# Cosine attention and a two-layer network in one kernel: the first eighteen pairs in another order, three loads in two parts, fewer products of zeros

## The chip, the cores and the metric

The kernel runs on one core of one Trainium2 chip. The metric is the time of one execution in microseconds (us), from the device. A core has five engines that run their own instruction queues in order: TensorE (PE, matrix products; its loads of the stationary operand are listed as PEld), VectorE (DVE), ScalarE (ACT), GpSimd (POOL) and SyncE (SP, which here only issues transfers). Sixteen DMA engines move data between HBM and SBUF.

## The reference

```python
q_n = q / (norm(q, axis=-1) + 1e-06);  k_n = k / (norm(k, axis=-1) + 1e-06)
scores = matmul(q_n, k_n.transpose(0, 1, 3, 2)) / tau
attn = softmax(scores)
x = matmul(attn, v)                      # (8, 12, 448, 64), then (3584, 768)
h = x @ w_in                             # (3584, 2048)
g = h * clip(h + 3.0, 0.0, 6.0) / 6.0
out = g @ w_out                          # (3584, 768)
```

Eight batches, twelve heads, 448 positions, head dimension 64, tau 0.1; all inputs and the output are float32.

## The kernel before

**Pairs.** Heads h and h+6 of a batch are a pair, so there are 48 pairs, six to a batch. An item is the queries or the keys of two neighbouring pairs: 128 partitions by 14 rows of 64 numbers (two heads by seven columns c). Items 0 to 13 alternate: item 0 is the queries of pairs 0 and 1, item 1 their keys, item 2 the queries of pairs 2 and 3, item 3 their keys, and so on. In all there are 48 items.

**Steps of an item.** LQ loads it (SP, 448 KB, `load_qk`, L199). SQ squares it by columns on POOL or ACT (L225, L227), RE sums the squares on DVE (L242); BN and BS do the same for a few columns on DVE by moments (L248, L253, L254). NO makes the inverse norms of an item or of both items of two pairs: Ln and Exp on ACT (L278, L279), then either Ln and Exp again on ACT (L284, L285) or, with "v", a sum and a reciprocal on DVE (L281, L282). NM multiplies the item by its inverse norms into bfloat16 (`normalise`, L295), whole or by heads (".0", ".1"), on DVE or POOL. TR transposes it on PE into a PSUM bank (L341), and CQ and CK copy queries and keys of one pair to SBUF, with CS for the last 64 keys (`copy`, L361 on ACT, L363 on DVE).

**Steps of a pair.** SC are the scores, products of keys and queries in four groups 0 to 3 (L441, L444). EX are the exponentials (ACT, L462): for pairs 0 to 5 one instruction of 896 columns for each of three groups and one of 448, from two double banks SC; from pair 6 on, where a ring of six single banks is opened (OPEN), seven of 448 columns. LV loads values (four transfers for two pairs, L214), VC casts them (L312 on DVE, L314 on POOL or ACT). VA multiplies with the values into the bank PV (L484), FI divides by the sums (DVE, L504, L505), BK transposes back (L518) and CX copies into x (L361, L363).

**The network.** W issues one load of weights from POOL's queue (L924). U issues a unit of the first layer (six products of 448 columns, L594) or of the second (L754, L834); UH issues a part of a first-layer unit of batch 0 while its pairs are still being made; UA and UV are the work on ACT and DVE behind a unit (L611, L617). GS and WS are sums that the second layer's scheme of fewer products needs.

**Products of zeros.** DP.n issues n products of a zero tile into unused columns of PV (248 columns, bfloat16, L937); DQ.n does so with the zeros taken as float32, which the trace lists as two records each; D.n uses 512 columns and the bank Y (L931). Nothing reads what they write.

**What sets the order.** The program for pairs 0 to 17 is written out by hand in `PLAN`, a list of such steps: `LQ.1` loads item 1, `SQ.1.p.3.2` squares two columns of item 1 from column 3 on POOL, `SC.6.0` is group 0 of pair 6. The instructions of each engine run in the order in which the plan names them, so a step that waits holds up all steps behind it on its engine. `run` reads the plan; from pair 18 on a loop sets the order, which the change leaves alone. Names ".Y" and ".Z" in the plan pick a PSUM bank; without them `bank_of` takes the next of the ring.

Of the kernel before, what the change touches and what calls it, by code (L numbers as in the profile page):

```python
# [64 lines left out]
def kernel(
# [125 lines left out]
    def load_qk(j, *heads):  # L191
        needs(("NM", raw_before(j)))
        raw_of[j] = raw_buffer(j)
        d = j // 2
# [4 lines left out]
        nc.sync.dma_start(out=raw_of[j][:, g, :, :].rearrange("p g c d -> p g (c d)"), in_=f[:, g, :])  # L199
# [16 lines left out]
    def square(j, e, c0, n):  # L216

        needs(("RE", j - 2), ("LQ", j, 0), ("LQ", j, 1))
        if j not in sq_of:
# [4 lines left out]
        if e == "a":
            nc.scalar.activation(out=o, in_=i, func=AF.Square)  # L225
# [29 lines left out]

    def norms(d, *items):
        on_vector, items = "v" in items, tuple(x for x in items if x != "v")
# [2 lines left out]
        items = items or (0, 1)  # L260
# [2 lines left out]
        it = slice(items[0], items[-1] + 1)
        inverse([t[:, d % 2, it, :] for t in n2_and_r], nr_eps[:, d % 2, it, :, :], on_vector)
# [3 lines left out]
    def norms_two(d, on_vector=None):  # L268

        needs(*(("NM", 2 * d + x) for x in range(-4, 0)), *(("RE", 2 * d + x) for x in range(4)))  # L270
        two = [t.rearrange("p e i c -> p (e i) c") for t in n2_and_r]
        inverse(two, nr_eps.rearrange("p e i c x -> p (e i) c x"), on_vector)
        issued.update(("NO", x, y) for x in (d, d + 1) for y in range(2))

    def inverse(tiles, pairs, on_vector):
# [3 lines left out]
        nc.scalar.activation(out=nr, in_=ln, func=AF.Exp, scale=0.5)  # L279
        if on_vector:  # L280
            nc.vector.tensor_reduce(out=le, in_=pairs, axis=AX.X, op=ALU.add)  # L281
            nc.vector.reciprocal(out=r, in_=le)  # L282
        else:
            nc.scalar.activation(out=le, in_=nr, func=AF.Ln, bias=eps_bias)  # L284
            nc.scalar.activation(out=r, in_=le, func=AF.Exp, scale=-1.0)  # L285

    def normalise(j, e, *heads):
# [7 lines left out]
        engines[e].tensor_tensor(  # L295
            out=nrm[:, :, g, :].rearrange("p c g d -> p g c d"),
            in0=raw_of[j][:, g, :, :],
            in1=n2_and_r[2][:, d % 2, j % 2, :]
            .rearrange("p (g c) -> p g c", g=2)[:, g, :]
            .to_broadcast([128, n, 7, D]),  # L300
# [18 lines left out]
    def bank_of(name, reads):  # L319

        bank = {"Y": Y, "Z": Z}[name] if name else next_bank()
# [796 lines left out]
```

## Time and profile before

| | us |
|---|---|
| median of 3 runs | 400.86 (400.78 to 400.98) |
| the profiled execution | 401.17 |
| its span, first to last instruction | 399.2 |
| busy in the span: PE / DVE / ACT / POOL | 390.2 / 293.9 / 276.9 / 234.6 |

The granted clock of TensorE was 1.000 over the span. A row of the timeline gives the start, the time from the start of the first to the end of the last of the merged instructions, engine, line, operation, tiles, form and count; in brackets stands the idle time of the engine before it, and what ended that. A row of busy time by stretch gives, for a stretch of the span, its length, then for each engine the busy time and the count of instructions. Lines are those of the kernel before; in the changed kernel the same code stands some 5 to 53 lines further down.

### The profile page before, as it was taken

The numbers are of one execution on the slowest core, as the hardware profiler recorded it, in microseconds if no ns is written. First come the engines' busy times: TensorE is split into PE (matmuls) and PEld (weight loads), VectorE is DVE, ScalarE is ACT, GpSimd is POOL, SyncE is SP. The second block draws the span as 40 slices with busy tenths as digits, with TensorE's granted clock in tenths as the row PEclk, the third lists the DMA queues.
The fourth block names the chain that finished last, engine by engine and source line by source line (L and its number), as shares of the span: only waits on it lengthen the run. The fifth ranks groups of instructions, "written<-read, shape, count | busy, mean of one in ns | idle before, by whom it ended". The sixth has DMA issues, their size and how long they took to land.

```text
span 399.2 us, 9590 instructions
## 1 busy us (share of the span) xinstructions
PE 390.2 (98%) x3658; PEld 231.6 (58%) x3658; DVE 293.9 (74%) x537; ACT 276.9 (69%) x600; POOL 234.6 (59%) x234
## 2 busy tenths in 40 slices
PE   7999999999999999999999999999999999999996
PEld 5566556555565556555565556565565556555563
DVE  7998898999777787667767886686756566645663
ACT  5999889895768677777868769668648755235230
POOL 6999628662656988389368757767666400400070
PEclk9999999999999999999999999999999999999999
DMA  8999979988978868785887566795953423230133
GB/s 289 310 221 240 212 226 248 199 189 208 197 172 187 120 174 162 174 213 123 195 202 213 136 152 155 165 218 119 190 150 69 102 48 68 47 74 20 30 71 97
DMA packets 93165, 63.73 MB, mean 160 GB/s; under 512 B 56128, under 2 KB 93120, under 8 KB 93120
## 3 DMA queue, kind: packets, MB, share of 16 engines
q1 hardware_dynamic: 87408, 56.45, 60.4%
q0 software_dynamic: 5312, 6.29, 9.4%
q8 instruction: 28, 0.46, 0.5%
q10 hardware_dynamic: 400, 0.39, 0.3%
q14 instruction: 17, 0.14, 0.1%
HBM read 45.61 MB, written 11.01 MB: 142 GB/s over the span
## 4 chain that ended last, share of the span: by engine, by line
PE 92%; ACT 3%; DVE 2%; DMA 1%; issue 0%; POOL 0%; SPq 0%; DVEq 0%; ACTq 0%
PE M L594 25%; PE M L754 17%; PE PV L484 11%; PE Z L594 6%; PE Y L754 6%; PE M L444 5%; PE Y L594 5%; PE Z L754 5%; PE M L834 3%; ACT at L462 2%; DMA big<-in_k_dram 1%; PE Y L444 1%; PE Z L444 1%; PE Z L834 1%; PE PV L937 1%; PE SC L444 1%
## 5 line engine op out<-in xcount | busy, mean ns | idle before, releaser
L594 PE MATMUL M<-xT,w_in_sb 128*128 128x448 bf16 x540 | 114.6, 353 | 0.0
L462 ACT ACTIVATE at<-M 128x448 bf16<-128x448 f32 x195 | 96.6, 564 | 20.0 <-PE M L444 10.2
L594 PEld LDWEIGHTS <-w_in_sb 128*128 128x128 bf16 x768 | 72.2, 98 | 64.1 <-issue 3.8
L227 POOL TENSOR_TENSOR big<-big 128x896 f32<-128x896 f32 (+5 forms) x47 | 69.5, 1483 | 21.7 <-DMA big<-in_k_dram 12.0
L295 POOL TENSOR_TENSOR nrm<-big,r 128x896 bf16<-128x896 f32 (+1 forms) x45 | 75.7, 1683 | 6.5 <-ACT r L285 4.3
L617 DVE SCALAR_TENSOR_TENSOR gT<-u,M 128x448 bf16<-128x448 bf16 x80 | 49.0, 619 | 34.9 <-ACT u L611 34.3
L611 ACT ACTIVATE u<-M,bias 128x448 bf16<-128x448 f32 x90 | 58.0, 651 | 22.3 <-PE M L594 20.9
L484 PEld LDWEIGHTS <-at 128*128 128x128 bf16 (+1 forms) x1536 | 53.8, 97 | 20.5 <-issue 10.6
L484 PE MATMUL PV<-vx,at 128*128 128x65 bf16 (+1 forms) x1536 | 62.2, 193 | 0.0
L242 DVE TENSOR_REDUCE n<-big 128x14 f32<-128x896 f32 (+1 forms) x48 | 51.1, 1068 | 1.5 <-POOL big L227 1.5
L783 POOL TENSOR_TENSOR big<-big 128x384 f32<-128x384 f32 x12 | 13.0, 1080 | 58.9 <-ACT big L802 58.8
L401 POOL COPY km<-tT 64x128 bf16<-64x128 bf16 x34 | 12.8, 376 | 59.0 <-DMA tT<-nrm 24.9
L754 PEld LDWEIGHTS <-gT 128*128 128x128 bf16 x320 | 30.9, 98 | 21.4
L505 DVE TENSOR_TENSOR on<-PV,rc 128x512 bf16<-128x512 f32 x48 | 33.2, 692 | 1.7
L754 PEld LDWEIGHTS <-gs 128*128 128x128 bf16 x248 | 23.9, 98 | 16.0 <-issue 0.2
L462 ACT ACTIVATE at<-Y 128x448 bf16<-128x448 f32 x51 | 28.7, 564 | 6.1 <-PE Z L444 6.0
L754 PE MATMUL M<-w_out_sb,gT 128*128 128x384 bf16 x176 | 32.2, 326 | 0.0
L444 PE MATMUL M<-tT,kz 64*128 64x448 bf16 (+1 forms) x175 | 31.6, 351 | 0.3 <-ACT at L462 0.3
L462 ACT ACTIVATE at<-Z 128x448 bf16<-128x448 f32 x48 | 26.9, 561 | 4.2 <-PE M L444 2.1
L754 PE MATMUL M<-w_sum,gs 128*128 128x384 bf16 (+1 forms) x168 | 29.1, 318 | 0.0
L594 PE MATMUL Z<-xT,w_in_sb 128*128 128x448 bf16 x132 | 28.6, 352 | 0.0
L729 DVE TENSOR_TENSOR gs<-gT 128x1024 bf16<-128x1024 bf16 x30 | 26.3, 876 | 0.0
(135 smaller groups left out, 562.3 us busy)
## 6 DMA issues: line engine op xcount, KB each, us to landing
big<-in_k_dram SPq DMA_DIRECT2D x24, 448.0 KB, 4.4
big<-in_q_dram SPq DMA_DIRECT2D x24, 448.0 KB, 4.4
out_dram<-o SPq DMA_DIRECT2D x107, 96.0 KB, 2.2
big<-in_v_dram SPq DMA_DIRECT2D x48, 128.0 KB, 4.1
big<-in_v_dram SPq DMA_DIRECT2D x48, 96.0 KB, 4.1
w_in_sb<-in_moe_w_in_dram POOLq DMA_DIRECT2D x8, 384.0 KB, 8.3
w_out_sb<-in_moe_w_out_dram POOLq DMA_DIRECT2D x4, 768.0 KB, 11.0
tT<-nrm SPq DMA_TRANSPOSE x34, 3.2
```

Of the source, the lines that this page charges most:

```text
L227: engines[e].tensor_tensor(out=o, in0=i, in1=i, op=ALU.mult)
L242: nc.vector.tensor_reduce(out=sums_of(j, c0, n), in_=sq[:, :, c0 : c0 + n, :], axis=AX.X, op=ALU.add)
L295: engines[e].tensor_tensor(out=nrm[:, :, g, :].rearrange("p c g d -> p g c d"), in0=raw_of[j][:, g, :, :], in1=n2_and_r[2][:, d % 2, j % 2, :]
L444: nc.tensor.matmul(o, ks, qt[rows], start=True, stop=True)
L462: nc.scalar.activation(out=o, in_=x, func=AF.Exp, scale=inv_tau)
L484: nc.tensor.matmul(pv_out(j, h), at[rows, n, q_cols(i // HP, j)], vt[rows, 3 + h if name == "M" else 5 * h + int(name[1]), :], start=(name ...
L505: nc.vector.tensor_tensor(out=on[:, :, :, :].rearrange("p j h d -> p h j d"), in0=pv4[:, :, :, 0:D], in1=rc[:, :, :].to_broadcast([128, 2, ...
L594: nc.tensor.matmul(ps[:, 0:S], w_in_sb[:, cc, fc * 128 : (fc + 1) * 128], xT[b % 2][:, cc, 0:S], start=(cc == 0), stop=(cc == CC - 1), ski ...
L611: nc.scalar.activation(out=u[:, :], in_=ps[:, 0:S], func=AF.Relu, bias=half_bias, scale=1.0 / 6.0)
L617: nc.vector.scalar_tensor_tensor(out=g[:, fc, c0 : c0 + S], in0=u[:, :], scalar=1.0, in1=ps[:, 0:S], op0=ALU.min, op1=ALU.mult,)
L729: nc.vector.tensor_tensor(out=o[:, :, :], in0=x, in1=y, op=op)
L754: nc.tensor.matmul(m, lhs[:, c, :], rhs[:, c, c0 : c0 + width], start=(base is None and c == 0), stop=(c == KC - 1), skip_group_check=True,)
```

## The change

The plan of pairs 0 to 17 is another one. What the diff below shows, in words:

- `load_qk` can load a part of the columns of an item (before: of its heads). Item 0 is loaded as columns 2 to 6 and then 0 and 1, item 3 as 4 to 6 and then 0 to 3, item 4 as 2 to 6 and then 0 and 1. Squares need only their own columns.
- NO is split into NA (the two steps on ACT) and NV (the other two), so that other work can stand between them.
- There are 9 products DP and 14 products DQ (before: 47 DP, 9 DQ, one D). All but four of them (DQ.1, DP.1 and DP.2 after the first scores) stand before the first scores; before, 40 of the DP stood behind them.
- Steps change engines, among others these. To ACT: all squares of items 1 (the columns not made by moments) and 5, the casts VC.5 and VC.8, CK.8, CX.2, the squares of items 16 (six columns) and 19. To DVE: CK.0, CQ.0, CX.0, VC.3, two columns of item 6 by moments. To POOL: half of NM.1, half of NM.2 and of NM.4, VC.0, NM.11, NM.12, more columns of item 15.
- The order of the whole list is another one. Among others NV.0.0, the inverse norms of item 0, stands behind SQ.2.a.0.4 on ACT; NM.1.p.0 and NM.0 follow each other on POOL; three weight loads W stand ahead of NM.6 and NM.7; UH.0.0 stands ahead of SC.7.1.
- `RING` writes out which PSUM bank each step takes, in place of the names in the plan.
- The code can also put inverse norms into PSUM for a `NM.w`; the plan has no such step.

```diff
 PLAN = [
-    "LQ.1 BN.1.0.3 DQ.9 SQ.1.p.3.2 SQ.1.a.5.2 BS.1.0.3 LQ.0 RE.1.3.4 SQ.0.p.0.3 LQ.3 SQ.3.p.0.4 SQ.0.a.3.4 RE.0 LQ.2",
-    "NO.0.1 NM.1.v.0 NM.1.v.1 SQ.3.a.4.3 NO.0.0 NM.0.p.1 SQ.2.a.4.3 TR.1.Z NM.0.p.0 LQ.5 SQ.2.a.0.4 D.1 DP.1 RE.3",
-    "CK.0.a SQ.5.p.0.4 SQ.5.a.4.3 RE.2 NO.1.v TR.0.Y LQ.4 CQ.0.a SQ.4.p.4.3 DP.2 SQ.4.a.0.4 DP.3 NM.3.p DP.1 RE.5",
-    "CQ.1.v RE.4 LV.0 SC.0.0.0 LQ.6 DP.3 VC.0.v NM.2.v.1 EX.0.0 SC.0.1.1 NM.2.p.0 CK.1.v LQ.7 LQ.8 DP.5 EX.0.1",
-    "SC.0.2.0 EX.0.2 DP.1 VC.1.v DP.1 DP.1 SC.0.3.1 EX.0.3 DP.2 VA.0.0 DP.2 LV.1 SQ.6.p.0.7 VA.0.1 SC.1.0.0 NO.2.v",
-    "NM.4.v.1 SC.1.1.1 TR.2.Y DP.1 NM.4.p.0 SQ.7.a.4.3 DP.1 RE.6 DP.1 DP.1 EX.1.0 EX.1.1 SC.1.2.0 TR.3.Z EX.1.2",
-    "CK.2.v DP.1 CQ.2.v SQ.7.p.0.4 DP.1 DP.1 VA.0.2 VA.0.3 SQ.8.a.4.3 NM.5.p SC.1.3.1 VC.3.p LQ.10 FI.0 EX.1.3 LQ.9",
...
-    "SC.3.2.0 DP.1 VA.2.2 VA.2.3 RE.9 SQ.11.p.0.7 CK.4.v NM.7.p EX.3.1 SC.3.3.1 EX.3.2 SC.4.0.0 EX.3.3 BK.0.Z FI.2",
-    "DP.1 RE.10 VA.3.0 W NO.4.v CK.5.v DP.1 RE.11 CX.0.a DP.2 LQ.12 SC.4.1.1 EX.4.0 TR.6.Z SC.4.2.0 NM.9.p VC.5.p W",
...
-    "CK.7.v VA.4.0 EX.5.3 VA.4.1 OPEN CS.7.v SC.6.0 EX.6.0 VA.4.2 VA.4.3.t CS.6.v FI.4 SC.6.1 EX.6.1 SC.6.2 SC.6.3",
...
+    "LQ.1 LQ.0.2.5 LQ.0.0.2 SQ.1.a.3.2 SQ.1.a.5.2 SQ.0.p.2.1 BN.1.0.3 LQ.3.4.3 SQ.0.p.0.2 RE.1.3.4 BS.1.0.3",
+    "SQ.0.a.3.4 RE.0.4.3 LQ.3.0.4 NA.0.1 RE.0.0.4 NV.0.1 LQ.2 LQ.5 SQ.3.a.0.4 SQ.3.p.4.3 NA.0.0 NM.1.v.1 SQ.2.a.0.4",
+    "NV.0.0 RE.3.0.4 SQ.2.a.4.3 LQ.4.2.5 NM.1.p.0 RE.2.0.3 DQ.10 DP.3 TR.1 RE.3.4.3 RE.2.3.4 CK.0.v CK.1.v NM.0.p",
+    "SQ.5.a.4.3 LQ.4.0.2 NA.1 NV.1.v SQ.4.a.0.4 SQ.5.a.0.4 LV.0 DQ.3 DP.1 TR.0 SQ.4.p.4.3 LQ.6 CQ.0.v RE.4 LQ.8",
+    "RE.5.0.7 LV.1 NM.3.p VC.1.v DP.2 SC.0.0.0 VC.0.p EX.0.0 SC.0.1.1 EX.0.1 DQ.1 DP.1 SC.0.2.0 TR.3 NM.2.p.0 EX.0.2",
+    "CQ.1.v NM.2.p.1 LQ.7 BN.6.0.2 BS.6.0.2 SQ.6.p.2.5 LV.2 NA.2 SC.0.3.1 NV.2.v VC.2.v VA.0.0 EX.0.3 CK.2.v SC.1.0.0",
+    "EX.1.0 DP.2 SC.1.1.1 VA.0.1 EX.1.1 SC.1.2.0 EX.1.2 TR.2 NM.4.p.1 SQ.7.p.0.4 VA.0.2 VA.0.3 CQ.2.v SQ.7.a.4.3",
...
+    "SC.2.3.1 RE.7.0.7 LQ.10 CQ.3.v VA.1.0 LQ.9 SQ.8.a.0.4 EX.2.2 VC.3.v TR.5 W VA.1.1 VA.1.2 EX.2.3 RE.8 SQ.9.a.0.4",
+    "SC.3.0.0 SQ.9.p.4.3 CK.4.v NA.3 W EX.3.0 VA.1.3.t LV.3 FI.1 RE.9 SQ.10.p.0.7 SC.3.1.1 TR.4 EX.3.1 CQ.5.v W",
+    "VA.2.0 LQ.11 NA.4 NV.3.v VA.2.1 CQ.4.v SC.3.2.0 VC.4.v SC.3.3.1 VA.2.2 EX.3.2 VA.2.3 EX.3.3 SC.4.0.0 SC.4.1.1",
+    "SQ.11.p.0.7 NM.6.p VC.5.a LQ.12 EX.4.0 FI.2 EX.4.1 VA.3.0 CK.5.v NM.7.p.1 BK.0 SC.4.2.0 VA.3.1 VA.3.2 EX.4.2",
+    "RE.11 BK.2 CX.2.a SC.4.3.1 VA.3.3.t SC.5.0.0 EX.4.3 EX.5.0 TR.6 NM.7.p.0 SC.5.1.1 RE.10 CX.0.v NV.4.v TR.7",
+    "EX.5.1 FI.3 CQ.7.v SC.5.2.0 EX.5.2 CK.6.v SC.5.3.1 EX.5.3 OPEN NA.5 VA.4.0 VA.4.1 VA.4.2 CQ.6.v LQ.13 VA.4.3.t",
+    "SC.6.0 CS.6.v SC.6.1 NM.8.p EX.6.0 CK.7.v EX.6.1 BK.3 CS.7.v SC.6.2 W BK.1 FI.4 EX.6.2 NV.5.v VA.5.0 CX.3.v",
...
-    def load_qk(j, *heads):
+    def load_qk(j, *part):
...
-        g = slice(heads[0], heads[0] + 1) if heads else slice(0, 2)
-        nc.sync.dma_start(out=raw_of[j][:, g, :, :].rearrange("p g c d -> p g (c d)"), in_=f[:, g, :])
+        c0, w = part or (0, 7)
+        o = raw_of[j][:, :, c0 : c0 + w, :].rearrange("p g c d -> p g (c d)")
+        nc.sync.dma_start(out=o, in_=f[:, :, c0 * D : (c0 + w) * D])
...
     def norms(d, *items):
+        norms_root(d, *items)
+        norms_inverse(d, *items)
...
+    def root(tiles, pairs):
         n2, le, r = tiles
         ln, nr = n2, pairs[:, :, :, 0]
         nc.scalar.activation(out=ln, in_=n2, func=AF.Ln)
         nc.scalar.activation(out=nr, in_=ln, func=AF.Exp, scale=0.5)
```

More of the change, by code (lines that the diff above doesn't have):

```diff
@@ L21 @@
 PLAN = [
[39 rows of a table removed]
-]
[40 rows of a table added]
+]
+PLANNED = " ".join(PLAN).split()
+RING = "232323322345012345012345012340123012345234501234501234012350123450123450123450123450123501234501345012345012345012345012345012345012345012345012"
 @with_exitstack
@@ L216, in square @@
     def square(j, e, c0, n):
-        needs(("RE", j - 2), ("LQ", j, 0), ("LQ", j, 1))
+        needs(("RE", j - 2), *(("LQ", j, c) for c in range(c0, c0 + n)))
         if j not in sq_of:
@@ L244, in moments @@
     def moments(j, c0, n):
-        needs(("RE", j - 2), ("LQ", j, 0), ("LQ", j, 1))
+        needs(("RE", j - 2), *(("LQ", j, c) for c in range(c0, c0 + n)))
         for c in range(c0, c0 + n):
@@ L254, in sums_of_moments, with norm_tiles, inverses, in_psum @@
         nc.vector.scalar_tensor_tensor(out=sums_of(j, c0, n), in0=mean, scalar=1.0, in1=m2, op0=ALU.mult, op1=ALU.add)
+    def norm_tiles(d, items):
+        items = tuple(x for x in items if x != "v") or (0, 1)
+        it = slice(items[0], items[-1] + 1)
+        return items, [t[:, d % 2, it, :] for t in n2_and_r], nr_eps[:, d % 2, it, :, :]
     def norms(d, *items):
[L257 removed]
+        norms_root(d, *items)
+        norms_inverse(d, *items)
+    def inverses(j, g):
+        n = j // 2 % 2 * 2 + j % 2
+        c = slice(7 * g, 7 * g + 7)
+        if any(x in PLANNED for x in (f"NM.{j}.w", f"NM.{j}.w.{g}")):
+            return PV[:, 1, 264 + 14 * n : 278 + 14 * n][:, c]
+        return n2_and_r[2][:, j // 2 % 2, j % 2, c]
+    def in_psum(j):
+        return [any(x in PLANNED for x in (f"NM.{j}.w", f"NM.{j}.w.{g}")) for g in range(2)]
+    def norms_root(d, *items):
         needs(("NM", 2 * d - 4), ("NM", 2 * d - 3))
[L260 removed]
+        items, tiles, pairs = norm_tiles(d, items)
         for x in items:
             needs(("RE", 2 * d + x))
[L263 to L264 removed]
+        root(tiles, pairs)
+    def norms_inverse(d, *args):
+        items, tiles, pairs = norm_tiles(d, args)
+        le, r = tiles[1:]
+        parts = [(le, r)]
+        if any(any(in_psum(2 * d + x)) for x in items):
+            parts = []
+            for n, x in enumerate(items):
+                h = in_psum(2 * d + x)
+                n7 = PV[:, 1, 264 + 14 * (d % 2 * 2 + x) : 278 + 14 * (d % 2 * 2 + x)]
+                if h[0] == h[1]:
+                    parts.append((le[:, n, :], n7 if h[0] else r[:, n, :]))
+                else:
+                    for g in (0, 1) if h[0] else (1, 0):
+                        c = slice(7 * g, 7 * g + 7)
+                        parts.append((le[:, n, c], n7[:, c] if h[g] else r[:, n, c]))
+        inverse(tiles, pairs, "v" in args, parts)
         for x in items:
@@ L270, in norms_two @@
         needs(*(("NM", 2 * d + x) for x in range(-4, 0)), *(("RE", 2 * d + x) for x in range(4)))
+        assert not any(any(in_psum(2 * d + x)) for x in range(4))
         two = [t.rearrange("p e i c -> p (e i) c") for t in n2_and_r]
-        inverse(two, nr_eps.rearrange("p e i c x -> p (e i) c x"), on_vector)
+        pairs = nr_eps.rearrange("p e i c x -> p (e i) c x")
+        root(two, pairs)
+        inverse(two, pairs, on_vector)
         issued.update(("NO", x, y) for x in (d, d + 1) for y in range(2))
-    def inverse(tiles, pairs, on_vector):
+    def root(tiles, pairs):
         n2, le, r = tiles
@@ L279, in inverse @@
         nc.scalar.activation(out=nr, in_=ln, func=AF.Exp, scale=0.5)
+    def inverse(tiles, pairs, on_vector, parts=None):
+        n2, le, r = tiles
+        nr = pairs[:, :, :, 0]
+        parts = parts or [(le, r)]
         if on_vector:
             nc.vector.tensor_reduce(out=le, in_=pairs, axis=AX.X, op=ALU.add)
-            nc.vector.reciprocal(out=r, in_=le)
         else:
             nc.scalar.activation(out=le, in_=nr, func=AF.Ln, bias=eps_bias)
-            nc.scalar.activation(out=r, in_=le, func=AF.Exp, scale=-1.0)
+        for x, o in parts:
+            if on_vector:
+                nc.vector.reciprocal(out=o, in_=x)
+            else:
+                nc.scalar.activation(out=o, in_=x, func=AF.Exp, scale=-1.0)
     def normalise(j, e, *heads):
@@ L294, in normalise @@
         n = len(heads)
+        assert e == "w" or not any(in_psum(j)[x] for x in heads)
+        if n == 1 or e == "w":
+            r = inverses(j, heads[0]) if n == 1 else PV[:, 1, 264 + 14 * (j % 4) : 278 + 14 * (j % 4)]
+        else:
+            r = n2_and_r[2][:, d % 2, j % 2, :]
         engines[e].tensor_tensor(
@@ L319, in bank_of @@
     def bank_of(name, reads):
[L321 removed]
+        bank = next_bank()
         key = id(bank)
@@ L924, in next_weights @@
         nc.gpsimd.dma_start(out=o, in_=w)
-    def busy(n):
-        bank_of("Y", 0)
-        for _ in range(n):
-            nc.tensor.matmul(Y[:, :], zeros[:, 0:128], zeros[:, :], start=True, stop=True)
     def busy_pv(n, z=None):
```

22 lines of the change are left out of this document (10 added, 12 removed), and 55 rows, old and new, of the table PLAN.

## The prediction

> **What bounds the kernel now.** I read the summary of the span first, then the table of busy time by stretch, then the early part of the timeline engine by engine, then the landing times of the first loads.
>
> ```profile
> span 399.2 us, 9590 instructions
> PE 390.2 (98%) x3658; PEld 231.6 (58%) x3658; DVE 293.9 (74%) x537; ACT 276.9 (69%) x600; POOL 234.6 (59%) x234
> ```
>
> TensorE (PE) is busy for nearly the whole span. But part of that is work that counts for nothing, the products of zeros at L937. The next two views part the stages: all instructions first, then L937 alone (columns: stretch, its length, busy PE, PEld, DVE, ACT, POOL with counts, granted clock, DMA share, GB/s; in the second only PE and PEld).
>
> ```profile
> 7.50:12.70 5.20, 2.83 (x27) 1.67 (x26) 4.61 (x7) 4.55 (x13) 4.93 (x5) 1.00 1.08 325
> 12.70:20.00 7.30, 7.18 (x84) 4.33 (x85) 7.20 (x15) 7.11 (x13) 7.30 (x7) 1.00 1.04 320
> 20.00:28.00 8.00, 7.65 (x115) 5.28 (x115) 7.77 (x17) 7.84 (x16) 7.98 (x7) 1.00 0.91 211
> 28.00:34.50 6.50, 5.81 (x89) 3.72 (x87) 6.25 (x19) 6.45 (x11) 6.48 (x7) 1.00 1.11 274
> 34.50:43.00 8.50, 8.38 (x163) 6.10 (x164) 6.18 (x21) 7.77 (x17) 8.48 (x11) 1.00 1.13 209
> 43.00:60.00 17.00, 16.93 (x166) 9.14 (x159) 16.02 (x32) 14.91 (x33) 6.35 (x6) 1.00 0.97 222
> 60.00:105.00 45.00, 44.95 (x445) 25.46 (x444) 41.89 (x76) 37.42 (x81) 27.58 (x27) 1.00 1.00 207
> ```
> ```profile
> 12.30:20.00 7.70, 3.51 (x22) 1.67 (x22) 1.00 1.04 322
> 20.00:28.00 8.00, 2.35 (x13) 1.03 (x13) 1.00 0.91 211
> 28.00:34.50 6.50, 0.80 (x5) 0.32 (x4) 1.00 1.11 274
> ```
>
> See three stages. Up to 12.7 us the engines wait for the first loads. From 12.7 to 34.5 us ScalarE (ACT) and GpSimd (POOL) have no idle time (21.4 of 21.8 us and 21.8 of 21.8 us) and VectorE (DVE) hardly any, while 6.7 us of PE's busy time is zeros. From 34.5 us PE is full with real work (8.38 of 8.50, 16.93 of 17.00, 44.95 of 45.00) and stays so. So the plan matters until about 36 us: the later pair 6 starts, the later the full stretch and the end, one for one. In the middle stage ACT sets the pace, from the first of the rows below to the last.
>
> ```profile
> 12.17 0.63 ACT L225 ACTIVATE big<-big 128x512 f32<-128x512 f32 x1
> 12.72 0.92 ACT L462 ACTIVATE at<-SC 128x896 bf16<-128x896 f32 x1
> 34.91 0.98 ACT L462 ACTIVATE at<-M 128x448 bf16<-128x448 f32 x2 [0.43 <-PE M L444]
> ```
>
> The first exponential starts at 12.72 us, that of pair 6 at 34.91 us, and the one wait worth naming between them is the 0.43 us before pair 6. My sum is therefore the shift of the first exponential, plus what ACT gets or loses up to pair 6, plus what the full stretch adds.
>
> **Change, part 1: the loads.** Six loads of 448 KB stand at the head of SP's queue. Items 0, 3 and 4 (first queries, second keys, third queries) are now two transfers each, so 256 more packets for the same bytes. Landings before (issue plus time to landing; the four rows are items 3, 2, 5, 4):
>
> ```profile
> 1.76 0.47 SPq L199 DMA_DIRECT2D big<-in_k_dram  x1
> 2.27 0.47 SPq L199 DMA_DIRECT2D big<-in_q_dram  x1
> 2.78 0.47 SPq L199 DMA_DIRECT2D big<-in_k_dram  x1
> 3.29 0.48 SPq L199 DMA_DIRECT2D big<-in_q_dram  x1
> ```
> ```profile
> big<-in_k_dram SPq DMA_DIRECT2D x1, 448.0 KB, 5.7
> big<-in_q_dram SPq DMA_DIRECT2D x1, 448.0 KB, 6.4
> big<-in_k_dram SPq DMA_DIRECT2D x1, 448.0 KB, 7.1
> big<-in_q_dram SPq DMA_DIRECT2D x1, 448.0 KB, 8.2
> ```
>
> That is 7.46, 8.67, 9.88 and 11.49 us: one per 1.2 us at the end of a full queue (DMA share 1.08 in 7.5 to 12.7 us above), so the 0.5 us that each extra issue costs SP is hidden, and packets are what counts. What a split load costs no row shows. The nearest is the load of values, also 448 KB in 512 packets: the queue moved 382 GB/s between 2.5 and 9 us with whole loads, 274 GB/s between 9.5 and 11.5 us with mostly values.
>
> ```profile
> DMA packets 1464, 2.48 MB, mean 382 GB/s; under 512 B 79, under 2 KB 1464, under 8 KB 1464
> DMA packets 623, 0.55 MB, mean 274 GB/s; under 512 B 74, under 2 KB 623, under 8 KB 623
> ```
>
> 458,752 bytes take 1.20 us at the one and 1.67 us at the other: 0.47 us for each split. Below, the bound is nothing (bytes alone count); above, I take twice that, 0.94 us. I use 0.47, the row of equal size and packet count. Item 3 then lands whole at 7.46 + 0.94 = 8.4, item 2 at 9.6, item 5 at 10.8, item 4 at 11.49 + 1.41 = 12.9 us. The first part of item 0 gains little: 320 KB in place of 448, 2/7 of 1.20 us, so 0.34 us at best, and nothing below hangs on it.
>
> The Trainium skill, "DMA: Bandwidth & Descriptors", section Specifications, puts the least transfer at line rate at 512 B. All parts here have runs of 512 B or more, so by that page a split is free; this case's own values, in runs of 768 and 1024 B, ran at 274 against 382 GB/s and speak against it. What it would do is the second rival.
>
> **Part 2: the way to the first exponential.** Durations before:
>
> ```profile
> 6.49 0.31 ACT L284 ACTIVATE le<-nr,bias 128x14 f32<-128x14 f32 x1
> 6.83 0.21 ACT L285 ACTIVATE r<-le 128x14 f32<-128x14 f32 x1
> 7.52 0.52 ACT L225 ACTIVATE big<-big 128x384 f32<-128x384 f32 x1 [0.48 <-DMA big<-in_k_dram]
> 9.06 1.98 POOL L295 TENSOR_TENSOR nrm<-big,r 128x448 bf16<-128x448 f32 x2 [0.20 <-ACT r L285]
> 19.64 1.68 POOL L295 TENSOR_TENSOR nrm<-big,r 128x896 bf16<-128x896 f32 x1
> 11.10 0.56 PE L341 MATMUL Y<-ident,nrm 128*128 128x128 bf16 x7 [0.81 <-POOL nrm L295]
> 12.32 0.36 PE L444 MATMUL SC<-tT,kz 64*128 64x448 bf16 x2
> 13.32 0.38 DVE L363 COPY tT<-Y 128x448 bf16<-128x448 bf16 x1
> ```
>
> Before, ACT squared part of item 3 when that landed (7.52 us) and then made the inverse norms of item 0, and POOL normalised item 0 at 9.06 us. In the new order of ACT the inverse of item 0 (NV.0.0) stands behind a square of item 3 and a square of item 2 (SQ.2.a.0.4), which waits for item 2. That is the added wait; queued behind it are NV.0.0 and, through it, POOL's NM.0 and all of POOL's later work. Step by step: item 3's square 8.4 to 9.05; NA.0.0 to 9.4; item 2's square from 9.6 to 10.25; NV.0.0 (0.31 + 0.21 and a hop) to 10.8; NM.0 in one piece, 1.68, to 12.5; transposes 0.56, the copy CQ.0 0.38 (now on DVE, not on ACT), the first scores 0.36, and four hops of 0.05: 14.0 us. The other way to the same point: item 4 lands at 12.9, then two squares of 512 columns (0.63, next start after 0.53) before the first exponential: 14.0 as well. So the first exponential moves from 12.72 to 14.0: **+1.3 us**. With free splits it is 13.05 (+0.3); at twice the price 14.9 (+2.2). Four columns of item 5's squares moved from POOL to ACT lie in the second way; CK.0 and CQ.0, now on DVE, leave ACT at a time when it now waits for loads.
>
> The zeros ahead of it: ten products of type f32 in place of nine, and three more of bf16, before the first transposes.
>
> ```profile
> 1.20 6.67 PE L937 MATMUL PV<-xT 128*128 128x248 f32 x18 [1.20 <-DVE xT L986]
> 11.50 0.80 PE L937 MATMUL PV<-xT 128*128 128x248 bf16 x6
> ```
>
> Twenty records at 6.67/18 and three at 0.80/6 end at 1.20 + 7.41 + 0.40 = 9.0 us; item 1 is normalised at about 9.3 (estimate: item 3's first part lands 4/7 of 1.67 us ahead of 8.4; POOL squares it, 6/14 of a whole item's 1.68 or a little more, and then normalises its half of item 1, 1.98/2), so they cost nothing; they would if item 1 came 0.3 us sooner.
>
> **Part 3: from the first exponential to pair 6.** ACT's squares of items 7, 8, 9, the roots of four pairs of items and one copy of x are the same before and after, in another order. New on ACT is the cast of values VC.5:
>
> ```profile
> L314 ACT CAST vx<-big x3: 631/633/663, 76.5 to 100.9; 128x512 bf16<-128x512 f32 x3
> ```
>
> 0.63 us, 0.1 of it overlapped: **+0.5**. The wait of 0.43 us before pair 6 was for a key copy at the end of a long run on DVE; with ACT later than DVE it may go, or POOL's delay may renew it: **-0.3**, between 0 and -0.43. The 36 products of zeros that vanish here (40 to 5, L937) lie on PE beside an ACT without idle time: nothing. If that cover were not there, see the first rival. Up to pair 6 DVE gives up three half normalisations, a cast and a copy and gets three copies, a cast and the moments of two columns, near balance; POOL is taken up in the third rival. RING only names banks in another order, NA and NV are the halves of NO, the path through PSUM is not used by this plan: nothing.
>
> **Part 4: from pair 6 on.** Same products on a full PE. Six first-layer products take 1.14 us, 1.24 where they follow scores:
>
> ```profile
> 64.45 1.14 PE M L594 x6
> 66.68 1.24 PE M L594 x6
> ```
>
> Ten such switches more or fewer are 1 us either way; I take 0. Squares of items 16 and 19 go from POOL to ACT, which has 7.6 us of idle time in 60 to 105: nothing.
>
> Sum: 1.3 + 0.5 - 0.3 = **+1.5 us**, a span of 400.7 us. The profiled execution took 401.17 us, 1.97 around its span and 0.31 over the median of 400.86; on the median the forecast is 402.4 us, its own range 401.7 to 403.3 (the upper end is the doubled price of a split).
>
> **The rivals.**
>
> First, faster: PE is the bound before 34.5 us too, since the chain runs through L937.
>
> ```profile
> PE M L594 25%; PE M L754 17%; PE PV L484 11%; PE Z L594 6%; PE Y L754 6%; PE M L444 5%; PE Y L594 5%; PE Z L754 5%; PE M L834 3%; ACT at L462 2%; DMA big<-in_k_dram 1%; PE Y L444 1%; PE Z L444 1%; PE Z L834 1%; PE PV L937 1%; PE SC L444 1%
> ```
>
> 1% of the span is 4.0 us; gone whole, it leaves 1.5 - 4.0 = -2.5: 398.4 us; by half, 400.4. It decides if scores reach ACT sooner once zeros no longer stand ahead of them. Against it: ACT is busy 21.4 of 21.8 us there and cannot take them sooner.
>
> Second, splits are free (the page's rule above): +0.3 + 0.5 - 0.3 = +0.5, 401.4 us, within 400.9 to 401.7. For it: the pieces are large. Against it: the values' rate.
>
> Third, POOL becomes the bound. It had no idle time from 12.7 to 43 us, its NM.0 now starts near 10.8 instead of 9.06, and three weight loads (W) stand ahead of NM.6 and NM.7 where one did.
>
> ```profile
> L924 POOL DMA_DIRECT2D w_in_sb<-in_moe_w_in_dram x8 | 5.7, 708 | 0.0
> ```
>
> So NM.7 ends 1.7 + 2 x 0.7 = 3.1 us later, 1.6 more than the rest. If pair 6 waits for all of it: 404.0 us; I put the middle at 403.4. Against it: before, POOL may have had that much in hand, since ACT was not waiting for it.
>
> Fourth, PE's clock drops when the zeros are gone. PE's real work in 20 to 34.5 us is 7.65 - 2.35 + 5.81 - 0.80 = 10.3 us; at half speed 20.6, about 6 us too much: 408 us. Against it: with 0.8 us of zeros in 28 to 34.5, 77% real work, the granted clock stayed 1.00. The Trainium skill, "TensorE: Matmul & The Clock Gate", section HAM oscillation, has the clock fall after idle gaps of more than about 3.4 us; the trace has none so long after 1.2 us, and I expect none.
>
> **How the numbers follow.** Forecast 0.47, first rival 0.15, second 0.20, third 0.13, fourth 0.05. The measurement can tell about 0.2% (0.8 us) from no change: faster 0.15, within it 0.20, slower 0.65. The range takes in forecast, second and third and the near end of the first: 399.8 to 404.0.
>
> **What would show it.** Right: the first exponential near 14.0 us behind a wait for item 4 or for scores, that of pair 6 near 36.4, item 2's square on ACT waiting for its load, ACT without idle time between, PE full from then. Wrong: items 2 and 4 landing at 8.7 and 11.5; ACT idle in the middle; PE less full after 36 us; a granted clock under 1.

## The result and the profile after

The changed kernel takes 403.20 us (median of 7 runs, 402.75 to 405.79) against 400.98 us (400.60 to 401.86) in the same set: **ratio 1.0065, 95% interval 1.004 to 1.009**, so slower by about 2.2 us. Its profiled execution took 403.77 us, with a span of 401.9 us (before: 401.17 and 399.2). Single executions of one kernel differ by 5 us and more (400.69 to 405.92 us for the kernel before beside one of the runs below), so the ratios with their intervals are the measure of time, and the profiles show where time goes. Three executions of one run below (item 9 ahead: 408.05, 409.89 and 410.21 us) were in a slow state and are left out of its row.

Busy time by stretch after (columns as in the prediction: stretch, length, busy PE, PEld, DVE, ACT, POOL, granted clock, DMA share, GB/s):

```profile
12.70:20.00 7.30, 5.91 (x69) 3.51 (x66) 6.93 (x14) 6.46 (x11) 6.17 (x7) 1.00 1.11 291
20.00:28.00 8.00, 5.75 (x74) 4.19 (x73) 6.36 (x13) 5.98 (x12) 5.68 (x7) 0.79 1.08 289
28.00:34.50 6.50, 5.38 (x79) 3.44 (x77) 5.63 (x14) 6.47 (x12) 6.49 (x6) 1.00 1.13 178
34.50:43.00 8.50, 7.74 (x119) 5.01 (x120) 6.72 (x23) 7.89 (x18) 8.49 (x9) 1.00 0.97 228
60.00:105.00 45.00, 45.00 (x436) 25.34 (x435) 41.84 (x75) 38.52 (x83) 24.43 (x26) 1.00 0.91 192
```

Before, ACT and POOL had hardly any idle time from 12.7 to 34.5 us. Now ACT works 5.98 of 8.00 us in 20 to 28 us and POOL 5.68; the clock is 0.79 there; and the DMA share is 1.11, 1.08 and 1.13 in the first three rows (before 1.04, 0.91 and 1.11). From 60 us PE is as full as before. The timeline of ACT after shows its long waits on the way to pair 6:

```profile
12.78 0.92 ACT L515 ACTIVATE at<-SC 128x896 bf16<-128x896 f32 x1 [0.34 <-PE SC L497]
...
19.27 0.52 ACT L230 ACTIVATE big<-big 128x384 f32<-128x384 f32 x1 [0.72 <-DMA big<-in_k_dram]
...
25.99 0.63 ACT L230 ACTIVATE big<-big 128x512 f32<-128x512 f32 x1 [1.99 <-DMA big<-in_k_dram]
...
36.00 1.35 ACT L515 ACTIVATE at<-SC 128x896 bf16<-128x896 f32 x2 [0.35 <-PE SC L497]
...
37.78 1.42 ACT L515 ACTIVATE at<-M 128x448 bf16<-128x448 f32 x3
```

The first exponential starts at 12.78 us (before 12.72) and that of pair 6 at 37.78 us (before 34.91): +2.87, all but 0.06 of it between the two. The same stretch as one row, before and then after:

```profile
12.70:34.90 22.20, 21.02 (x287) 13.49 (x288) 21.59 (x52) 21.40 (x38) 22.16 (x19) 1.00 1.02 265
```
```profile
12.80:37.80 25.00, 19.57 (x265) 12.82 (x263) 21.78 (x51) 21.76 (x39) 21.55 (x21) 0.93 1.06 253
```

ACT's work grew by 0.36 us (21.40 to 21.76), its idle time by 2.44 (0.80 to 3.24). From pair 6 to the end it is 364.1 us now, 364.3 before. So the loss, but for 0.36 us, is idle time of ACT ahead of pair 6, and the two waits for the key loads of items 7 and 9 in the timeline above come to 2.71 us. POOL waits for item 9 too:

```profile
26.06 0.82 POOL L232 TENSOR_TENSOR big<-big 128x384 f32<-128x384 f32 x1 [2.30 <-DMA big<-in_k_dram]
```

SP's issues, before and then after, show why these loads come late:

```profile
11.07 0.37 SPq L199 DMA_DIRECT2D big<-in_k_dram  x1
11.54 0.42 SPq L199 DMA_DIRECT2D big<-in_q_dram  x1
12.01 2.56 SPq L214 DMA_DIRECT2D big<-in_v_dram  x4
14.68 0.54 SPq L199 DMA_DIRECT2D big<-in_q_dram  x1
16.00 3.06 SPq L199 DMA_DIRECT2D big<-in_k_dram  x2
19.12 4.08 SPq L214 DMA_DIRECT2D big<-in_v_dram  x5
```
```profile
9.65 0.37 SPq L205 DMA_DIRECT2D big<-in_q_dram  x1
10.66 2.56 SPq L219 DMA_DIRECT2D big<-in_v_dram  x4
13.32 0.54 SPq L205 DMA_DIRECT2D big<-in_k_dram  x1
13.90 3.22 SPq L219 DMA_DIRECT2D big<-in_v_dram  x4
17.23 0.53 SPq L205 DMA_DIRECT2D big<-in_q_dram  x1
17.87 0.41 SPq L205 DMA_DIRECT2D big<-in_k_dram  x1
18.37 3.91 SPq L219 DMA_DIRECT2D big<-in_v_dram  x4
22.39 0.53 SPq L205 DMA_DIRECT2D big<-in_k_dram  x1
```

Item 7 was issued at 11.07, ahead of the values LV.1; now at 13.32, behind them. Item 9 was issued at 16.00, with no values LV.2 ahead of it; now at 17.87, behind LV.2. Item 11 follows at 22.39 (before: the second of the two at 16.00, 18.70). And item 9 takes longer from issue to landing (before, then after): 5.6 and 8.0 us. It lands at 25.9 instead of 21.7 us.

```profile
big<-in_k_dram SPq DMA_DIRECT2D x1, 448.0 KB, 5.6
```
```profile
big<-in_k_dram SPq DMA_DIRECT2D x1, 448.0 KB, 8.0
```

The clock has a row of its own. Stretches of 3.41 us after, cut where the clock changes:

```profile
16.25:19.67 3.42, 2.55 (x39) 1.65 (x39) 3.12 (x7) 2.70 (x4) 2.29 (x3) 1.00 1.10 270
19.67:23.08 3.41, 1.62 (x18) 0.77 (x16) 3.38 (x8) 3.41 (x7) 3.41 (x4) 1.00 1.08 320
23.08:26.49 3.41, 3.41 (x42) 2.68 (x43) 2.22 (x5) 1.42 (x3) 1.11 (x2) 0.50 1.09 250
26.49:29.91 3.42, 2.09 (x41) 1.65 (x39) 2.87 (x7) 3.36 (x9) 3.40 (x5) 1.00 1.20 248
```

PE was busy 1.62 of 3.41 us (48%); in the next 3.41 us it ran at half clock. ACT waited for item 9 from 24.0 to 26.0 us, inside that time. The fall is not needed for the loss: one of the seven executions of the changed kernel had a mean granted clock of 1.000 (a fall of 3.41 us makes it 0.996), and it took 403.20 us, which is the median.

### The profile page after: what moved, and what is told of

Read it like the earlier page. It is cut to its first block, busy times and chain, and to the rows that moved or that the text cites. A ratio compares the mean times of both kernels' runs of the same rounds, so it can differ in the third digit from the quotient of the medians.

```text
span 401.9 us, 9550 instructions
## 1 busy us (share of the span) xinstructions
PE 389.7 (97%) x3629; PEld 232.2 (58%) x3629; DVE 292.5 (73%) x540; ACT 278.0 (69%) x602; POOL 235.6 (59%) x238
## 4 chain that ended last, share of the span: by engine, by line
PE 89%; DMA 3%; POOL 3%; SPq 2%; ACT 1%; issue 1%; DVE 0%; POOLq 0%; ACTq 0%
PE M L647 24%; PE M L807 19%; PE PV L537 11%; PE Z L647 7%; PE Y L647 6%; PE M L497 5%; PE Y L807 5%; PE Z L807 4%; PE M L887 3%; DMA big<-in_k_dram 2%; PE Y L497 1%; DMA big<-in_v_dram 1%; PE Y L887 1%; PE Z L497 1%; POOL big L232 1%; SPq L205 1%
## 5 line engine op out<-in xcount | busy, mean ns | idle before, releaser
L647 PE MATMUL M<-xT,w_in_sb 128*128 128x448 bf16 x510 | 108.3, 353 | 0.3 <-DVE xT L416 0.3
L350 POOL TENSOR_TENSOR nrm<-big,r 128x896 bf16<-128x896 f32 (+1 forms) x51 | 80.4, 1581 | 13.9 <-ACT r L335 7.9
L232 POOL TENSOR_TENSOR big<-big 128x896 f32<-128x896 f32 (+5 forms) x46 | 65.6, 1427 | 15.0 <-DMA big<-in_k_dram 8.7
L664 ACT ACTIVATE u<-M,bias 128x448 bf16<-128x448 f32 x85 | 55.0, 652 | 23.3 <-PE M L647 22.6
L537 PEld LDWEIGHTS <-at 128*128 128x128 bf16 (+1 forms) x1536 | 53.4, 97 | 21.2 <-issue 12.7
L670 DVE SCALAR_TENSOR_TENSOR gT<-u,M 128x448 bf16<-128x448 bf16 x75 | 45.9, 618 | 27.1 <-ACT u L664 26.4
L247 DVE TENSOR_REDUCE n<-big 128x14 f32<-128x896 f32 (+3 forms) x52 | 51.1, 994 | 4.2 <-POOL big L232 3.3
L807 PE MATMUL M<-w_out_sb,gT 128*128 128x384 bf16 x192 | 35.0, 326 | 0.0
L807 PE MATMUL M<-w_sum,gs 128*128 128x384 bf16 (+1 forms) x192 | 33.5, 319 | 0.0
L515 ACT ACTIVATE at<-Z 128x448 bf16<-128x448 f32 x52 | 29.3, 564 | 4.3 <-PE M L497 4.3
L367 POOL CAST vx<-big 128x512 bf16<-128x512 f32 x37 | 25.8, 698 | 1.6 <-DMA big<-in_v_dram 1.5
```

The lines of the kernel that those rows point to most:

```text
L247: nc.vector.tensor_reduce(out=sums_of(j, c0, n), in_=sq[:, :, c0 : c0 + n, :], axis=AX.X, op=ALU.add)
L350: engines[e].tensor_tensor(out=nrm[:, :, g, :].rearrange("p c g d -> p g c d"), in0=raw_of[j][:, g, :, :], in1=r.rearrange("p (g c) -> p g ...
L367: (engines[e].copy if e == "a" else engines[e].tensor_copy)(out=o, in_=f)
L515: nc.scalar.activation(out=o, in_=x, func=AF.Exp, scale=inv_tau)
L537: nc.tensor.matmul(pv_out(j, h), at[rows, n, q_cols(i // HP, j)], vt[rows, 3 + h if name == "M" else 5 * h + int(name[1]), :], start=(name ...
L647: nc.tensor.matmul(ps[:, 0:S], w_in_sb[:, cc, fc * 128 : (fc + 1) * 128], xT[b % 2][:, cc, 0:S], start=(cc == 0), stop=(cc == CC - 1), ski ...
```

## Experiments

**Theory T:** the delay is late transfers (items 7, 9 and 11 behind values and weights in a full queue) and, in their cover, the clock's fall. Theory L of the first expectations is its first half alone. **Rivals:** W, the waits only take up slack; Q, each transfer moved forward makes another one late; C, the clock alone; O, the order of the loads alone; N, zeros cost the time that they take on PE; P, the new order of steps costs by itself; F (against the prediction's price), splits are free. Plan diffs are cut to the steps around the edit, several steps to a line. For each run: median with lowest and highest, ratio to the kernel before measured beside it (whose medians went from 400.98 to 402.51 us) with its interval, and from its profile the start of the first exponential and of pair 6.

| run | us | ratio to before | first / pair 6 |
|---|---|---|---|
| changed kernel | 403.20 (402.75 to 405.79) | 1.0065 [1.0040, 1.0090] | 12.78 / 37.78 |
| item 7 ahead | 405.31 (403.00 to 407.03) | 1.0073 [1.0040, 1.0106] | 13.46 / 39.10 |
| item 9 ahead | 403.56 (402.00 to 407.22) | 1.0057 [1.0023, 1.0090] | 13.08 / 38.19 |
| items 7 and 9 ahead | 403.65 (402.42 to 407.75) | 1.0056 [1.0025, 1.0088] | 12.80 / 37.26 |
| whole loads | 403.34 (402.94 to 406.99) | 1.0056 [1.0029, 1.0083] | 12.67 / 36.66 |
| zeros back | 405.01 (404.53 to 407.30) | 1.0081 [1.0052, 1.0111] | 12.67 / 37.90 |
| loads in time | 405.45 (404.64 to 407.43) | 1.0093 [1.0065, 1.0121] | 12.70 / 39.33 |
| loads in time, zeros | 406.79 (405.14 to 410.21) | 1.0132 [1.0077, 1.0186] | 14.45 / 41.38 |
| before, no zeros | 402.13 (400.29 to 404.16) | 1.0002 [0.9971, 1.0032] | 12.69 / 34.98 |
| transfers back, weights late | 405.42 (404.25 to 408.39) | 1.0072 [1.0047, 1.0097] | 12.87 / 38.70 |
| before, new transfers | 404.92 (403.18 to 408.20) | 1.0070 [1.0039, 1.0102] | 14.62 / 42.10 |
| before, split loads | 402.36 (400.77 to 404.33) | 0.9981 [0.9953, 1.0009] | 14.57 / 36.58 |
| all three | 403.34 (401.60 to 406.18) | 1.0027 [0.9994, 1.0061] | 12.66 / 35.42 |

In four of these profiles the first loads landed late (item 4 complete at 12.2, 13.4, 13.1 and 13.4 us in item 7 ahead; loads in time, zeros; before, new transfers; before, split loads; 10.9 to 11.7 elsewhere), and in the last two the clock was also at half, from 11.46 to 14.88 and from 10.39 to 13.80 us. One of the four loads them whole, so it takes no split to be late; what delays them stays open. Of these profiles, take the difference between the two starts.

### The price of a split

Undone in the changed kernel, and made alone in the kernel before (there with the changed `load_qk`, and squares and moments that need only their columns):

```diff
-LQ.0.2.5 LQ.0.0.2
+LQ.0
...
-LQ.3.4.3
+LQ.3
...
-LQ.3.0.4
...
-LQ.4.2.5
+LQ.4
...
-LQ.4.0.2
```

> The changed kernel with items 0, 3 and 4 each loaded whole, each at the place of its first part; nothing else moved. The prediction's price of a split (0.47 us each, 1.3 us at the first exponential): the first exponential comes near 11.5 us instead of 12.8 and the time falls to 401.9. Theory F (splits are free, the packets of 512 B take about half the time of those of 1 KB): item 2 lands within 0.3 us of the changed kernel's 8.35, the first exponential comes at 12.8 to 13.2, and the time is 403.2 to 403.6.

> The kernel before with items 0, 3 and 4 loaded in two parts each as in the changed kernel; nothing else. The prediction's price (0.47 us each): item 4 lands at 12.9 us, the first exponential comes near 14.0 us, 402.1 us. Theory F (splits are free): item 4 lands within 0.3 us of 11.5, the first exponential within 0.3 us of 12.7, 401.0 to 401.5.

Measured: split loads in the kernel before give 0.9981, whose upper end 1.0009 leaves room for 0.4 us, not for 1.3. In the changed kernel whole loads leave the first exponential where it was, 12.67 against 12.78. **So F holds as far as it can be told:** no price of a split shows at the first exponential or in the time of the kernel before. (The profile of the split-load run is one of the four with late first loads and says nothing on the price.) The ratios of the changed kernel with whole and with split loads, 1.0056 and 1.0065, are too uncertain to tell 1 us. In the profile with whole loads pair 6 starts 1.1 us sooner: SP has three issues fewer, item 9 went out at 17.15 us in place of 17.87 and landed at 24.4. Two of its twelve executions had a mean clock of 1.000 and took 403.30 and 403.39 us, again the middle of the set.

### The transfers' order in the kernel before

```diff
-LQ.7 LQ.8
+LQ.8 LV.1 LQ.7 LV.2
...
-LV.1
...
 LQ.10 FI.0 EX.1.3 LQ.9
+LV.3
 SC.2.0.0 LQ.11
+LQ.12
...
-LV.3
...
-LV.2
...
-LV.4
...
-LQ.12
...
 LQ.13
+LV.4
```

> The kernel before with SP's transfers in the order of the changed kernel (LQ.8, LV.1, LQ.7, LV.2, LQ.10, LQ.9, LV.3, LQ.11, LQ.12, later LV.4); steps on all other engines, zeros and weight loads stay. Theory T: items 7, 9 and 11 land near 19, 25 and 28 us instead of 15.4, 21.7 and 23.0; GpSimd and ScalarE wait 2 us or more for them, pair 6 near 37 us, 403 us or more. Theory P: the kernel before has the time in hand, under 0.8 us lost: 401.2 to 402.

1.0070: the order of SP's transfers alone, with every other step and all zeros of the kernel before, costs as much as the whole change. The clock fell in it too (mean 0.996 or less in all ten executions; at half from 21.70 to 28.53 us in the profile), so the 0.7% includes whatever that adds. Its profiled execution is the longest of its ten, but it shows where. ACT's timeline (first rows), POOL's (last):

```profile
14.62 3.16 ACT L462 ACTIVATE at<-SC 128x896 bf16<-128x896 f32 x4 [0.67 <-PE SC L444]
21.11 0.52 ACT L225 ACTIVATE big<-big 128x384 f32<-128x384 f32 x1 [2.95 <-DMA big<-in_k_dram]
25.96 1.41 ACT L462 ACTIVATE at<-SC 128x448 bf16<-128x448 f32 x2 [1.50 <-PE SC L441]
...
42.10 0.98 ACT L462 ACTIVATE at<-M 128x448 bf16<-128x448 f32 x2 [0.43 <-PE M L444]
```
```profile
27.91 0.82 POOL L227 TENSOR_TENSOR big<-big 128x384 f32<-128x384 f32 x1 [2.72 <-DMA big<-in_k_dram]
```

Item 7 holds ACT for 2.95 us and item 9 holds POOL for 2.72, as T says; W and P (for this kernel) fall.

### The loads' order in the changed kernel

Item 7 ahead, item 9 ahead, both (the first diff and the second), and loads in time (both, with the third):

```diff
 LQ.6 CQ.0.v RE.4 LQ.8
+LQ.7
 RE.5.0.7 LV.1
...
-LQ.7
```
```diff
-LV.2
+LQ.10 LQ.9 LV.2
...
-LQ.10
...
-LQ.9
```
```diff
-VC.2.v
...
 NM.4.p.0
+LQ.11 LV.2
...
+VC.2.v
 VC.3.v
...
-LV.3
...
-LQ.11
...
 LQ.12
+LV.3
```

> The changed kernel with the load of item 7 (LQ.7) issued ahead of the values LV.1, behind LQ.8; nothing else moved. Theory L (in the changed kernel ScalarE and GpSimd wait in the middle for items 7 and 9, whose loads are issued behind value loads): LQ.7 is issued near 11.3 us, when NM.0 has freed its buffer, and lands near 15.5 instead of 19.2; the 0.72 us that ScalarE waits for it go, the 1.99 us wait for item 9 stays: 402.5 us, ratio to the changed kernel 0.998. Rival W (the stage is as long as the work of ScalarE and GpSimd in it, the waits only take up slack): 403.2, no change within 0.4.

> The changed kernel with the loads of items 10 and 9 issued ahead of the values LV.2, behind LQ.7; nothing else moved. Theory L: LQ.9 is issued near 16.2 us, as soon as NM.2 has freed its buffer (17.87 in the changed kernel), and lands near 22 instead of 25.9; the 1.99 us that ScalarE waits for it go, the 0.72 us for item 7 stay; pair 6 starts about 2 us sooner: 401.2 us. Rival W: 403.2, no change within 0.4. Rival Q (the DMA queue is full, so that item 9 lands no sooner than the bytes ahead of it allow, or the values then come late): item 9 lands after 24 us or the value casts wait, under 0.8 us gained: 402.5 or more.

> Both moves together: LQ.7 ahead of LV.1, LQ.10 and LQ.9 ahead of LV.2. Theory L: both waits go, 2.7 us in all, what is left against the kernel before is the cast VC.5 on ScalarE (+0.5) less what splits gain: 400.5 us, about equal to the kernel before. Rival W: 403.2 within 0.4. Rival Q: a wait of the same size for values (VC.3 or VC.5, or a score's wait for another item) takes their place: 402.5 or more.

> The changed kernel with the loads in the order of their use: item 7 ahead of values LV.1, items 10, 9 and 11 ahead of values LV.2, item 12 ahead of LV.3; the cast VC.2, which has until about 26 us, moves on VectorE from ahead of the copy CK.2 to just ahead of VC.3, so that it waits for no value. No zeros. Theory T: items 7, 9 and 11 land near 16.5, 21 and 24 us and no wait for them is over 0.3 us, but the clock falls for 3.41 us or more as before, and scores come late: 402 to 403.5. Rival O (the order of the loads alone is the cause): 401.0 or less. Rival Q (another transfer is now the late one): 403 or more, with a wait for values or weights.

None gives the time back (1.0056 to 1.0093): L's times miss in the first three, T's 402 to 403.5 in the last (405.45). None of the four has the whole old order, so O is not tried in full, but moving these loads alone does not mend it. By the times alone W would do as well as Q; the profiles decide: the waits named above go and others come. With items 7 and 9 ahead, one wait of DVE for values and two of ACT for scores:

```profile
18.45 0.69 DVE L365 TENSOR_REDUCE vx<-big 128x512 bf16<-128x512 f32 x1 [0.61 <-DMA big<-in_v_dram]
```
```profile
20.19 0.92 ACT L515 ACTIVATE at<-SC 128x896 bf16<-128x896 f32 x1 [0.79 <-PE SC L497]
...
25.59 0.92 ACT L515 ACTIVATE at<-SC 128x896 bf16<-128x896 f32 x1 [0.61 <-PE SC L497]
```

Now LV.1 comes late: VC.2 waits for it with the copies CK.2 and CQ.2 behind it on DVE, and the scores of pair 2 need these (0.79). Then the clock is at half from 22.50 to 25.91 us and the scores of pair 3 are late (0.61). With loads in time pair 2 starts at 19.17 us, 0.9 sooner than in the kernel before, and then LV.2, which shares the DMA engines with the early weight loads and item 12, is the late one; the cast VC.5 holds ACT and VC.4 holds DVE:

```profile
30.35 0.62 ACT L367 CAST vx<-big 128x512 bf16<-128x512 f32 x1 [1.76 <-DMA big<-in_v_dram]
```
```profile
30.39 0.69 DVE L365 TENSOR_REDUCE vx<-big 128x512 bf16<-128x512 f32 x1 [2.53 <-DMA big<-in_v_dram]
```

Q is what these runs show: in a full queue, moving one transfer forward only names another that is late.

### The zeros

The kernel before without 39 of its 40 products behind the first scores (the expectation counts 38); the changed kernel with 37 put back (zeros back), the same with loads in time (loads in time, zeros), and 19 of them with loads in time and three weight loads later (transfers back, weights late; its W as in the last run below):

```diff
-DP.3
...
-DP.5
...
```
```diff
-VA.0.2 VA.0.3 CQ.2.v
+VA.0.2 DP.3 VA.0.3 CQ.2.v
...
-SC.1.3.1 SC.2.0.0
+SC.1.3.1 DP.7 SC.2.0.0 DP.6
...
-SC.2.1.1
+SC.2.1.1 DP.6
...
```

> The kernel before without the 38 products DP between the first scores and the opening of the ring; nothing else. First rival of the prediction (zeros stand on the chain): 400.4 to 398.4. Its main line (zeros lie beside a busy ScalarE): 400.9 with no change within 0.3. Theory T: PE is busy about 60% in 12 to 20 us and 66% in 20 to 28 us, near the edge at which the clock fell (48 to 56% busy), so that it falls in some executions, and each fall costs 0 to 2 us: median 401 to 403, with a wider spread than the kernel before.

> The changed kernel with 37 products of zeros (DP) put back between 18 and 35 us, where TensorE waits; loads as in the changed kernel. The trace of the changed kernel shows TensorE's clock at half from 23.08 to 26.49 us, behind a stretch of the same 3.41 us in which PE was busy 48%; the three experiments before fell behind stretches of 28 to 56%. Theory T (two causes that cover each other: late loads of items 7, 9 and 11, and the clock's fall; either alone gives most of the delay): the clock stays at 1.00 after 12 us, ScalarE still waits for item 9, 403.2 us in most executions, with fewer above 404. Rival C (the clock alone is the cause): 401.0. Rival N (zeros cost what they take on PE): 37 x 0.13 = 4.8 us, up to 408.

> Both: loads in the order of their use, and the 37 products of zeros. Theory T: no fall of the clock after 12 us, no wait for loads over 0.3 us; what is left against the kernel before is VC.5 on ScalarE, +0.5, and free splits: pair 6 near 35 to 35.5 us, 401.0 to 401.5. If the delay comes from elsewhere (work moved to ScalarE and POOL, weights loaded sooner): 402.5 or more.

> The changed kernel with its transfers put back near the order of the kernel before: loads in the order of their use as in the run with loads in time (VC.2 moved likewise), the three early weight loads W behind the square of item 11, NM.6 and NM.7 on GpSimd (so that they no longer share the DMA engines with items 11 and 12 and values LV.2), and 19 products of zeros between 18 and 23 us only. Theory T (the transfers' order and the clock are the whole delay): no wait of ScalarE over 0.4 us for a load or a value, clock 1.00 after 12 us in most executions, pair 6 near 35.4 us, 401.0 to 401.5 us. Theory P (the order of steps on the engines costs by itself: a wait of one engine for another takes the place of each that is removed): pair 6 at 37 us or later, 403 us or more.

Without these zeros the kernel before stays at 1.0002, and pair 6 starts at 34.98 (34.91): the interval leaves room for 1.2 us less, where the first rival wanted 2 to 4, so that rival is out. N falls with it for this kernel: 39 products of 0.13 us would be 5 us. But the clock of this run falls behind a stretch in which PE worked 1.78 of 3.41 us:

```profile
11.77:15.18 3.41, 1.78 (x13) 0.89 (x12) 3.29 (x7) 3.41 (x7) 3.41 (x4) 1.00 1.05 359
15.18:18.59 3.41, 3.29 (x31) 1.89 (x31) 3.34 (x8) 2.95 (x7) 3.41 (x3) 0.50 1.09 279
```

The mean granted clock was 0.996 or less in 8 of its 12 executions, in 8 of 29 of the kernel before beside it. In this profile ACT waits 0.43 us for scores within the half speed, and pair 6 comes no later for it.

Zeros put back do hold the clock at 1.00 (zeros back), and the waits for keys stay, so these are not the clock's doing:

```profile
POOL big L232 <- DMA big<-in_k_dram: 2.1, 1, 2.1
...
ACT big L230 <- DMA big<-in_k_dram: 1.2, 1, 1.2
```

Its 405.01 us does not judge C, which gave 401.0, because these three runs carry a fault of mine: the zeros are written to the bank PV, and FI.0 reads that bank; zeros that stand ahead of FI.0 in the plan hold it. C falls by the executions without a fall of the clock, 403.20 us for the changed kernel and 403.30 and 403.39 with whole loads. Transfers back, weights late, on DVE:

```profile
21.69 0.21 DVE L557 RECIPROCAL rc<-PV 128x8 f32<-128x8 f32 x1 [2.23 <-PE PV L985]
```

Behind FI.0 stand the sums RE.7 and RE.8, and POOL's and ACT's squares wait for those. So the times of the three runs say nothing against T or for it; the kernel before has no zeros between VA.0.3 and FI.0.

### All three

```diff
 LQ.6 CQ.0.v RE.4 LQ.8
+LQ.7
...
 VA.0.2 VA.0.3 CQ.2.v
+FI.0
 SQ.7.a.4.3 SC.1.3.1 SC.2.0.0
+DP.8
 NM.4.p.0
+LQ.11 LV.2
...
 SC.2.1.1
+DP.6
 NM.5.p SQ.8.a.4.3 CK.3.v
+VC.2.v
...
-VC.3.v
...
 RE.8
+VC.3.v
...
-W
...
-W
...
-W
...
 SQ.11.p.0.7
+W
 NM.6.p
+W
...
 TR.6 NM.7.p.0
+W
```

(LQ.10, LQ.9 and LV.3 stand as in loads in time; the old places of the moved steps are not all shown.)

> As the run with transfers put back and weights late, mended where that run's own zeros did harm: its zeros, written to the bank PV, stood ahead of FI.0, which waited 2.2 us for them on VectorE and held the squares' sums of items 7 and 8 and with them GpSimd and ScalarE. Here FI.0 stands right behind VA.0.3, the zeros (8 and 6) behind it, VC.2 behind CK.3 and VC.3 behind the sum of item 8. Theory T (late transfers and the clock are the delay): ScalarE waits less than 1 us in all between the first exponential (12.8) and pair 6, which starts at 35.0 to 35.6 us; no fall of the clock after 12 us; 401.0 to 401.5 us. Theory P (the new order of steps costs by itself): pair 6 at 36.5 us or later, 402.5 us or more, with ScalarE or GpSimd waiting for another engine and not for a transfer.

The stretch up to pair 6 as one row, and the two rows of ACT's timeline from 12.5 us to pair 6 that show a wait:

```profile
12.70:35.40 22.70, 19.59 (x279) 12.78 (x277) 21.36 (x50) 21.71 (x38) 20.86 (x20) 1.00 0.93 241
```
```profile
12.66 2.54 ACT L515 ACTIVATE at<-SC 128x896 bf16<-128x896 f32 x3 [0.52 <-PE SC L497]
...
33.63 1.35 ACT L515 ACTIVATE at<-SC 128x896 bf16<-128x896 f32 x2 [0.60 <-PE SC L497]
```

Pair 6 starts at 35.42 us, 2.36 sooner than in the changed kernel and inside T's 35.0 to 35.6; ACT's idle time is back to 0.99 us, none of it for a transfer; the clock is 1.00; item 9 lands at 21.1 us. Of the 2.36 us 1.0 is given back at 82.3 us, where PE waits for a DMA that transposes an item:

```profile
PE M L497 <- DMA tT<-nrm: 1.0, 1, 1.0
```

So its span is 400.8 us and its ratio 1.0027 [0.9994, 1.0061], which touches both no change and the changed kernel's interval. Its median of 403.34 us (beside it 401.56) misses T's 401.0 to 401.5 and lies where P had put it, though at pair 6 P missed. That the mended order gives pair 6 back is shown by one profile; that it gives the time back is not shown by the times, and where its other executions lose theirs stays open. Several things moved at once here, and which of them gives pair 6 back is not separated. It does not beat the kernel before.

## Why the prediction was right or wrong, step by step

- **Base: right.** From pair 6 to the end it is 364.3 us before and 364.1 after: between these two the end follows pair 6 one for one. (Over all profiles it is 364.1 to 366.0.)
- **Part 1, 0.47 us for a split: wrong.** No run shows a price. Item 2 landed at 8.4 us (forecast 9.6), item 4 at 11.3 (12.9). Its nearest row, the loads of values, misled me: a split load has as many packets and does not show their low rate, so the number of packets is not its cause; what is stays open. The second rival had this price right, but not the time (401.4).
- **Part 2, the first exponential +1.3: mis-sized with it,** +0.06 measured. That zeros ahead of the first transposes cost nothing was right.
- **Part 3, from the first exponential to pair 6, +0.5 and -0.3: this is the step that failed.** ACT's work grew by 0.36, near the +0.5 for VC.5 (which no run tests alone), and the wait of 0.43 went as I said. But "the same before and after, in another order" took the order to be free, and I worked out the landing of the first six loads only. Items 7 and 9, moved behind values in SP's queue, cost ACT 2.71 us of waiting, 2.44 more idle time in all. The same order put into the kernel before costs 0.7%.
- **The vanished zeros, nothing: right for the time** (1.0002 without them); they did hold the clock, which the forecast had left to its fourth rival.
- **Part 4, nothing: right,** -0.2.
- The sum, +1.5 by +1.3, +0.5 and -0.3, thus came near +2.7 in the span by luck, with its largest term at nothing and another, of about twice its size, missing. Of the signs of being wrong three came: items 2 and 4 landed early, ACT stood idle in the middle, and the clock fell under 1.
- **Rivals.** The first (zeros on the chain) fell. The third (POOL as the bound) named 403.4 to 404.0, nearest to what was measured and by luck too: POOL itself stands idle 3.45 of 25.00 us, 2.30 of it for item 9. The fourth, the clock, came true as a fact and not as a price: half speed for 3.41 us, where I had put all the real work of 20 to 34.5 us, 10.3 us, at half speed; and it lay in the cover of the wait for item 9. An execution without it took as long (403.20 us). What it costs where no late load covers it was not separated: with items 7 and 9 moved forward the scores that came late in its time made ACT wait 0.61 us.
